# Block attention and a two-layer MLP: five rounds of 8, 8, 8, 6 and 6 token tiles in place of six of 6, W2 read from DRAM in each round, another order of products in a group

## Chip, cores, metric

One core of a Trainium2 chip runs the kernel. The metric is the time of one execution on the device in microseconds; lower is better.

## What is computed

Attention with a block-causal mask (blocks of 64 positions; 8 batches of 8 heads, 576 positions, head size 64), then layer norm, an MLP 512 -> 2048 -> 512 with ReLU, and the residual, in fp32:

```python
scores = scale * np.matmul(q, k.transpose(0, 1, 3, 2))
scores = np.where(block_i >= block_j, scores, -1000000000.0)
attn = np.exp(scores - np.max(scores, axis=-1, keepdims=True))
attn = attn / (np.sum(attn, axis=-1, keepdims=True) + 1e-09)
x = np.matmul(attn, v) ... reshaped to (8, 576, 512)
xn = (x - mu) / np.sqrt(var + 1e-06) * g_ln
out = x + np.maximum(xn @ w_ch1, 0.0) @ w_ch2
```

## The kernel before

The program is a list of tasks with dependencies, engines, estimated costs and priorities. `Plan.run` plays it through once while the kernel is built: at each moment every engine takes the ready task of lowest priority number whose buffers are free, and its instructions are emitted in that order. On the chip each engine then works through its own list in order; a task that waits holds up everything behind it on that engine. All loads and stores are issued from one list too, that of SyncE (SP). Buffers come from pools shared by several kinds of tile: `big`, `mid` and `small` (4, 9 and 15 buffers), with a most for each kind.

*Attention.* 32 pairs of heads (`pair`, priority 100 + 10 k). Per pair TensorE makes the scores (L394), VectorE adds the mask and takes the minimum (L409), ScalarE takes the exponential (L412), TensorE transposes the result (L421), a copy by ScalarE or VectorE (L216, L218) brings it to SBUF, TensorE multiplies by V (L427, L431), VectorE transposes (L504) and SyncE stores to the DRAM tensor `xd`. Four times `first` does the first 64 positions of eight pairs.

*Weights.* They arrive as 64-bit words; `decode` makes fp32 of them, 16 blocks of W1 and 16 of W2, from pair 12 on, the last ones well after attention. W1 goes to DRAM as fp32 (`w1f`); W2 is split into a high and a low part (two fp32r tiles whose sum is the weight) that stay in SBUF as `w2h` and `w2l`, 64 KB of each partition.

*Norm.* `norm_tiles(n, q)` takes two token tiles of 128: loads x from `xd` in four DMAs each, scales (L635), stores the row for the residual (L639), takes mean and variance (L644, L645), refines 1/sqrt on GpSimd (L662 and on), scales (L670, L673), transposes through VectorE and DRAM (L675, L679, L683) into `xt`. `operands(n)` forms from the three `xt` of a round the seven left operands `xm` of a seven-product scheme for a 2 x 2 block product, each split into high and low (L700 differences, L711 low parts).

*MLP.* 36 token tiles in six rounds of six. A round's tiles form two halves of three (384 tokens). Eight groups per round, each 256 hidden columns. In a group `products` computes the first layer by seven block products, 6 matmuls of 128x384 each, 42 in all (L803), from `wa` (products 1, 5, 2, 6) and `wb` (3, 7, 4). Products accumulate in three PSUM banks: `a` takes 1, 6, 7, 4, `d` takes 5, 3, `b` takes 2. ScalarE copies intermediate states to SBUF tiles t (L811), VectorE adds a later state to them (L816), then ScalarE (L822) and VectorE (L823) take the ReLU and split it into `h`. Product 4 continues in bank `a` and so waits until the addition to t5, which reads product 7 there, has ended. `second` multiplies `h` of the group before by W2, six matmuls 128x512 per token tile (L862), into a bank `y`, and VectorE adds it to the running sum `ya` (L871). The places of all these in a group are priorities written out by hand:

```python
p1 0, p5 14, p2 28, p6 30, p3 44, p7 58, p4 90
second: (7, 21, 37, 51, 65, 75)
```

`stream` brings `wa` and `wb`: in round 0 it builds them from `w1f` (GpSimd sums L762, splits L773) and stores them to `was` and `wbs`; in the later rounds it loads them, two buffers each. The norm work of round n + 1 runs under round n, gated by the first `h` of round n; that of round 0 runs under attention with the priority of pair 24 and no gate.

Of the kernel before, what the change touches and what calls it, by code (L numbers as in the profile page):

```python
# [26 lines left out]
TILES = 36  # L27
ROUND = 6
TN = 384
D_0, D_1 = 12.0, .97  # L30
LN_0 = 24
# [148 lines left out]
def pool(n):  # L180
    return .07 + n / 440

@with_exitstack
def attn_mlp_kernel(ctx: ExitStack, tc: tile.TileContext, qk, qk0, v, v0, w1, w2, g, out):
# [85 lines left out]
    new_v, new_word = mid("v", [P, 5, P], F32, 2), mid("wr", [P, 1024], I32, 2)  # L270
    new_h, new_xt = mid("h", [P, 2, 512], F32R, 6), mid("xt", [P, 2, 512], F32, 3)
# [3 lines left out]
    new_ya, new_x, new_xnt = (small(n, [P, 512], F32, k) for n, k in (("ya", 6), ("x", 2), ("xnt", 1)))  # L275
    new_t, new_tt, new_sum = small("t", [P, TN], F32, 4), small("tt", [P, 2, 2, P], F32, 3), small("sum", [P, 2, 256], F32, 2)
# [4 lines left out]
    w1f = [kind("w1f", [P, 2, 512], F32, NJ // 2, dram)() for _ in range(NJ // 2)]  # L281
    was, wbs = ([kind(n, [P, k], F32, NJ // 2, dram)() for _ in range(NJ // 2)] for n, k in (("was", 2048), ("wbs", 1536)))
# [4 lines left out]
    new_wf = kind("wf", [P, 2, 512], F32, 2, odd, "raw")  # L287
# [27 lines left out]
    w2b, w1b = {}, {}  # L315

    def decode(j, second, prio, gate):
# [29 lines left out]
        if not second:  # L347
            out = Buf(parent=w1f[j // 2])
            load(P * 2048, lambda: nc.sync.dma_start(out=w1f[j // 2].t[:, j % 2], in_=w()), r=[full], w=[out], prio=prio)
            w1b.setdefault(j // 2, []).append(out)  # L350
            return
        whole = w2s[j // 4]
        hb, lb = (Buf(parent=x) for x in whole)
        add(any_of(lambda e: copy(e, whole[0].t[:, j % 4], w()), ACT=act(n, True), DVE=.12 + n / 1920),
            r=[full], w=[hb], prio=prio)
        add(any_of(lambda e: e.tensor_sub(whole[1].t[:, j % 4], w(), whole[0].t[:, j % 4]), POOL=pool(n)),
            r=[full, hb], w=[lb], prio=prio)
        w2b[j] = [hb, lb]
# [243 lines left out]
    ROUNDS = TILES // ROUND  # L602
    HALF_R = ROUND // 2
# [4 lines left out]
    def norm_tiles(n, q, prio, gate):  # L608
# [4 lines left out]
        for h in range(2):  # L613
            t = ROUND * n + HALF_R * h + q
# [76 lines left out]
    def operands(n, prio):  # L691

        tts = [new_tt() for _ in range(HALF_R)]
# [24 lines left out]
        Q = range(HALF_R)  # L718
# [23 lines left out]
    def stream(n, gp):  # L742

        wa, wb = new_wa(), new_wb()
        if n == 0 and gp < 2:
            for x in (wa, wb):
                x.after.extend(big_of[NPAIR - 1, z] for z in range(2))
        if n:
            load(P * 8192, lambda: nc.sync.dma_start(
                out=wa.t.rearrange("p a b c -> p (a b c)").bitcast(F32), in_=was[gp].t), r=[stored[gp, 0]], w=[wa], prio=3)  # L750
            load(P * 6144, lambda: nc.sync.dma_start(
                out=wb.t.rearrange("p a b c -> p (a b c)").bitcast(F32), in_=wbs[gp].t), r=[stored[gp, 1]], w=[wb], prio=3)
            return (wa, [wa]), (wb, [wb])
# [125 lines left out]
    for n in range(ROUNDS):  # L879
# [68 lines left out]
```

## Time and profile before

| | |
|---|---|
| median of 3 runs | 1107.7 us (1102.53, 1107.7, 1108.54) |
| profiled execution | 1102.45 us, its span 1100.7 us, mean granted clock 0.994 |
| busy share of the span | TensorE 97%, VectorE 73%, ScalarE 42%, GpSimd 25% |
| matmuls of the MLP | 2016 of 128x384 (L803), 1728 of 128x512 (L862) |
| DMA | 213.32 MB, 62% of 16 engines' span |

The busy time of TensorE counts overlapping matmuls from start to modelled end, so it says that the engine had work, not at what pace; the pace is read from the starts of matmuls. The span is that of the profiled execution, and the time beside it includes what lies around the program.

### The profile page before, as it was taken

The page shows a single profiled execution, that of the slowest core. Times are in us where ns is not written, and L with a number is a line of the kernel's source. Part 1 is how long each engine was busy: PE and PEld are TensorE (multiplying, and loading weights), DVE is VectorE, ACT ScalarE, POOL GpSimd, SP SyncE. Part 2 cuts the span into 40 slices and gives each one's busy share as a digit, 9 for nine tenths or more (in the row PEclk, how much of TensorE's full clock was granted, in tenths as well). Part 3 has the DMA queues.
Part 4 walks back from the last instruction along what each step waited for, and adds up shares of the span by engine and source line. Part 5 has one row for each costly group of instructions (what it writes and reads, how often), then busy time and mean ns, then how long its engine had stood idle before and what let it go on. Part 6 is the DMA issues. An engine that isn't in the chain of part 4 may idle for free.

```text
span 1100.7 us, 18673 instructions
## 1 busy us (share of the span) xinstructions
PE 1065.7 (97%) x6576; PEld 902.7 (82%) x6576; DVE 804.1 (73%) x1797; ACT 464.0 (42%) x1154; POOL 275.2 (25%) x428
## 2 busy tenths in 40 slices
PE   9999999999989899999999999999999999999998
PEld 6777666777779788888889878888898888899887
DVE  6878988888889899776686665867667676754554
ACT  7778888898864332322132212321223221322221
POOL 0013726232265662212220212212201122200000
PEclk9999999999999999999999999999999999999999
DMA  5559696966678758777637675376665676463311
GB/s 182 152 174 248 228 241 227 288 210 201 216 280 269 214 167 249 229 209 190 210 121 258 171 203 154 132 249 179 180 197 169 220 186 185 160 228 116 134 68 58
DMA packets 232174, 213.32 MB, mean 194 GB/s; under 512 B 158736, under 2 KB 187408, under 8 KB 225936
## 3 DMA queue, kind: packets, MB, share of 16 engines
q1 hardware_dynamic: 232080, 212.12, 62.2%
q8 instruction: 52, 0.85, 0.3%
q14 instruction: 42, 0.34, 0.1%
HBM read 155.45 MB, written 56.62 MB: 193 GB/s over the span
## 4 chain that ended last, share of the span: by engine, by line
PE 56%; DVE 20%; DMA 9%; SPq 4%; issue 4%; ACT 3%; POOL 2%; DVEq 0%; POOLq 0%; ACTq 0%
PE y L862 21%; PE p L803 20%; PE s L394 4%; PE o L431 4%; PE tr L421 4%; DMA xt<-xw 3%; DMA x<-xd 3%; DVE ya L871 3%; DVE xm L711 2%; PE o L427 2%; DVE h L823 2%; DVE t L816 2%; DVE pab L409 2%; SPq L679 1%; DVE x L670 1%
## 5 line engine op out<-in xcount | busy, mean ns | idle before, releaser
L862 PE MATMUL y<-w2h,h 128*128 128x512 f32 x1152 | 398.8, 394 | 0.0
L871 DVE TENSOR_TENSOR ya<-y,ya 128x512 f32<-128x512 f32 x288 | 197.0, 684 | 115.2 <-PE y L862 114.9
L862 PEld LDWEIGHTS y<-w2h,h 128*128 128x128 f32 x1152 | 217.7, 189 | 39.1
L862 PE MATMUL y<-w2l,h 128*128 128x512 f32 x576 | 228.2, 396 | 0.0
L803 PE MATMUL p<-xm,wa 128*128 128x384 f32 x1152 | 225.4, 337 | 0.6 <-DVE ot L504 0.6
L822 ACT ACTIVATE h<-t 128x384 fp32r<-128x384 f32 x144 | 75.6, 525 | 336.0 <-DVE t L816 336.0
L803 PEld LDWEIGHTS p<-xm,wa 128*128 128x128 f32 x1152 | 205.3, 189 | 9.6 <-DVE ot L504 0.9
L803 PE MATMUL p<-xm,wb 128*128 128x384 f32 x864 | 176.6, 339 | 17.3 <-DVE t L816 12.9
L803 PEld LDWEIGHTS p<-xm,wb 128*128 128x128 f32 x864 | 153.6, 188 | 35.2 <-DVE t L816 19.3
L862 PEld LDWEIGHTS y<-w2l,h 128*128 128x128 f32 x576 | 108.7, 189 | 15.9
L811 ACT COPY t<-p 128x384 f32<-128x384 f32 x144 | 68.6, 476 | 116.8 <-PE p L803 104.2
L394 PE MATMUL s<-raw 64*128 64x320 f32 (+4 forms) x640 | 96.4, 437 | 1.7 <-DVE ot L504 0.8
L823 DVE SCALAR_TENSOR_TENSOR h<-t,h 128x384 fp32r<-128x384 f32 x144 | 81.9, 569 | 22.0 <-ACT h L822 21.9
L816 DVE TENSOR_TENSOR t<-p,t 128x384 f32<-128x384 f32 x144 | 79.1, 550 | 21.4 <-PE p L803 20.9
L412 ACT ACTIVATE pab<-pab,nm 128x576 f32<-128x576 f32 (+1 forms) x128 | 91.4, 725 | 4.1 <-DVE nm L409 4.0
L394 PEld LDWEIGHTS s<-raw 64*128 64x128 f32 x640 | 61.2, 188 | 37.7 <-issue 29.1
L409 DVE CUSTOM_DVE_ANT_0 pab<-s,never 128x576 f32<-128x576 f32 (+1 forms) x128 | 82.9, 683 | 3.5 <-PE s L394 3.0
L431 PE MATMUL o<-pt,v 128*64 128x256 f32 (+1 forms) x768 | 81.4, 347 | 0.0
L431 PEld LDWEIGHTS o<-pt,v 128*64 128x64 f32 x768 | 57.2, 139 | 27.2 <-issue 1.1
L412 ACT ACTIVATE pu<-pu,nm 128x320 f32<-128x320 f32 (+1 forms) x128 | 64.0, 503 | 28.9 <-DVE nm L409 27.6
L662 POOL TENSOR_TENSOR norm<-norm 128x2 f32<-128x2 f32 x54 | 12.4, 229 | 254.5 <-DVE norm L656 251.6
L421 PE MATMUL tr<-ident,pab 128*128 128x128 f32 x512 | 66.9, 276 | 9.1 <-ACT pt L216 4.9
(91 smaller groups left out, 1142.1 us busy)
## 6 DMA issues: line engine op xcount, KB each, us to landing
wa<-was SPq DMA_DIRECT2D x40, 1024.0 KB, 6.2
wb<-wbs SPq DMA_DIRECT2D x40, 768.0 KB, 5.0
raw<-qk SPq DMA_DIRECT2D x32, 576.0 KB, 4.5
wr<-w SPq DMA_DIRECT2D x32, 512.0 KB, 5.7
v<-v SPq DMA_DIRECT2D x32, 320.0 KB, 4.3
x<-xd SPq DMA_DIRECT2D x144, 64.0 KB, 3.0
xrow<-x SPq DMA_DIRECT2D x36, 256.0 KB, 4.1
xw<-xnt SPq DMA_DIRECT2D x144, 64.0 KB, 3.3
```

What stands on the lines that cost most here:

```text
L394: nc.tensor.matmul(x, raw.t[HALF[h], 0, col], raw.t[HALF[h], 1, at:at + x.shape[1]], start=True, stop=True)
L409: add("DVE", dve(n) + .01, lambda: nc.vector.tensor_tensor_reduce(out=p.t[:, part(i, h)], in0=s.t[:, cols], in1=hide, scale=-0.125, scalar ...
L412: add("ACT", act(n, True) + .14, lambda: nc.scalar.activation(out=p.t[:, part(i, h)], in_=p.t[:, part(i, h)], func=AF.Exp, bias=nm.t[:, at ...
L421: nc.tensor.transpose(o.t[:, n * P:(n + 1) * P], x, ident)
L431: nc.tensor.matmul(o.t[HALF[h], at + lo:at + 256], v_sb.t[:, ck, HALF[h]], rhs(h), start=False, stop=(n == len(steps) - 1), skip_group_che ...
L803: nc.tensor.matmul(x.t[:, 0:TN], w_(l), xs[m].t[:, :, o, k], start=start and k == e == 0, stop=k == 1 and e == 2, skip_group_check=True)
L811: add("ACT", act(TN), lambda: nc.scalar.copy(out=t.t, in_=x.t[:, 0:TN]), r=[r], w=[new], prio=0)
L816: add("DVE", dve(TN), lambda: nc.vector.tensor_add(t.t, x.t[:, 0:TN], t.t), r=r, w=[new], prio=0)
L822: add("ACT", act(TN, True), lambda: nc.scalar.activation(out=x.t[:, 0, 0:TN], in_=src(), func=AF.Relu), r=r, w=[hi], prio=0)
L823: add("DVE", dve(TN), lambda: nc.vector.scalar_tensor_tensor(out=x.t[:, 1, 0:TN], in0=src(), scalar=0.0, in1=x.t[:, 0, 0:TN], op0=ALU.max, ...
L862: nc.tensor.matmul(y, x.t[:, l, at:at + P], w.t[:, j % 4], start=i == e == 0, stop=i == 1 and e == 2)
L871: add("DVE", dve(512), lambda yb=yb, ya=ya: nc.vector.tensor_add(ya.t, yb.t, ya.t), r=[part, was_], w=[now], prio=1)
```

## The change

The 36 token tiles are taken in five rounds of 8, 8, 8, 6 and 6, so that a half is 512 tokens in three rounds and 384 in two. W2's high and low parts are no longer kept in SBUF: `decode` stores them to a DRAM tensor `wcs`, and `stream` loads a tile `wc` of 1 MB for each group of each round, with two buffers. The room that this frees goes to the pools (6, 13 and 21 buffers in place of 4, 9 and 15, shared by more kinds), to wider `xm`, and to more `ya`, `xt`, `xnt` and `tt`. In a group product 2 moves from third to sixth place, and the places of the second product are given for 6 and 8 tiles. The norm work of round 0 gets gates and priorities of its own, one pair of tiles at each of the pairs of heads 10, 13, 16 and 19. The loads of `w1f` for round 0 wait for earlier pairs, the first group's `wa` and `wb` need no longer wait for the last pair's buffers, and the very first product waits for the last pair's scores.

```diff
-ROUND = 6
-TN = 384
+ROUNDS = 8, 8, 8, 6, 6
-LN_0 = 24
+LN_0, LN_1 = 10, 3
...
-        return kind(name, shape, dtype, 4, None, "big", most)
+        return kind(name, shape, dtype, 6, None, "big", most)
...
-        return kind(name, shape, dtype, 9, None, "mid", most)
+        return kind(name, shape, dtype, 13, None, "mid", most)
...
-        return kind(name, shape, dtype, 15, None, "small", most)
+        return kind(name, shape, dtype, 21, None, "small", most)
+    new_wc = big("wc", [P, 2, 2, DM], F32R, 2)
+    new_wf, new_wd = mid("wf", [P, 2, 512], F32, 2), mid("wd", [P, 2, DM], F32R, 2)
-    new_h, new_xt = mid("h", [P, 2, 512], F32R, 6), mid("xt", [P, 2, 512], F32, 3)
+    new_h, new_xt = mid("h", [P, 2, 512], F32R, 6), mid("xt", [P, 2, 512], F32, 4)
-    new_ya, new_x, new_xnt = (small(n, [P, 512], F32, k) for n, k in (("ya", 6), ("x", 2), ("xnt", 1)))
+    new_ya, new_x, new_xnt = (small(n, [P, 512], F32, k) for n, k in (("ya", 10), ("x", 2), ("xnt", 2)))
-    w2s = [[kind(f"w2{x}{q}", [P, 4, DM], F32R, 1)() for x in "hl"] for q in range(4)]
-    xs = [kind(f"xm{p}", [P, ROUND // 2, 2, 2, P], F32R, 1)() for p in range(7)]
+    xs = [kind(f"xm{p}", [P, max(ROUNDS) // 2, 2, 2, P], F32R, 1)() for p in range(7)]
...
+        if second:
+            wd = new_wd()
+            hi, lo = Buf(parent=wd), Buf(parent=wd)
+            add(any_of(lambda e: copy(e, wd.t[:, 0], w()), ACT=act(n, True), DVE=.12 + n / 1920),
+                r=[full], w=[hi], prio=prio)
+            add("POOL", pool(n), lambda: nc.gpsimd.tensor_sub(wd.t[:, 1], w(), wd.t[:, 0]), r=[full, hi], w=[lo], prio=prio)
+            load(P * 4096, lambda: nc.sync.dma_start(
+                out=to.t[:, 1024 * (j % 2):1024 * (j % 2) + 1024], in_=wd.t.rearrange("p l n -> p (l n)").bitcast(F32)),
+                r=[hi, lo], w=[out], prio=prio)
...
-        wa, wb = new_wa(), new_wb()
+        wa, wb, wc = new_wa(), new_wb(), new_wc()
         if n == 0 and gp < 2:
-            for x in (wa, wb):
+            for x in (wa, wb, wc)[0 if gp else 2:]:
                 x.after.extend(big_of[NPAIR - 1, z] for z in range(2))
...
         if n:
+            for k in range(3):
+                fetch(k, 3)
+            return [(x, [x]) for x in (wa, wb, wc)]
...
-        load(P * 4096, lambda: nc.sync.dma_start(out=wf.t, in_=w1f[gp].t), r=[*w1b[gp], *late], w=[wf], prio=prio)
+        load(P * 4096, lambda: nc.sync.dma_start(out=wf.t.rearrange("p a n -> p (a n)"), in_=w1f[gp].t),
+             r=[*whole[False, gp], ends[NPAIR - 6 + gp % 2]], w=[wf], prio=prio)
+        fetch(2, 3)
...
-        p1 = product(1, a, True, [], [], 0)
+        p1 = product(1, a, True, [ends[NPAIR - 1]] if n == gp == 0 else [], [], 0)
         k1 = keep(t1, a, p1)
         p5 = product(5, d, True, [], [], 14)
         k5 = keep(t5, d, p5)
-        p2 = product(2, b, True, [], [], 28)
-        c11 = plus(b, t1, [p2, k1])
-        done[0, 0] = finish(0, 0, lambda: t1.t, [c11])
-        p6 = product(6, a, False, [p1], [p1], 30)
+        p6 = product(6, a, False, [p1], [p1], 28)
         k6 = keep(t6, a, p6)
-        p3 = product(3, d, False, [p5], [p5], 44)
+        p3 = product(3, d, False, [p5], [p5], 42)
...
-        p7 = product(7, a, False, [p6], [p6], 58)
+        p7 = product(7, a, False, [p6], [p6], 56)
...
-        p4 = product(4, a, False, [p7], [p7], 90)
+        p2 = product(2, b, True, [], [], 70)
+        c11 = plus(b, t1, [p2, k1])
+        done[0, 0] = finish(0, 0, lambda: t1.t[:, 0:TN], [c11])
+        p4 = product(4, a, False, [p7], [p7], 84)
...
+    PLACES = {6: (7, 21, 35, 49, 63, 77), 8: (7, 21, 35, 49, 61, 65, 77, 91)}
...
-                gate = hs[0, 0][1]
+                gate = hs[0][0, 1][1]
```

## Rows read from the trace of the kernel before

**Rows 1.** Busy time of each engine in six stretches of the execution (us from the start): the window, its length, then for each engine the busy us and in brackets the instructions; then the granted TensorE clock as a share of 2.4 GHz, the busy share of the 16 DMA engines and what they moved in GB/s. 103 to 320 lies in the attention part, 320 to 447 is round 0, 576 to 705 round 2, 834 to 962 round 4, 962 to 1088 the last round.
```profile
103.00:215.00 112.00, 104.96 (x1010) 75.78 (x1008) 99.53 (x287) 95.38 (x262) 55.99 (x68) 0.98 0.82 250
215.00:320.00 105.00, 101.77 (x947) 75.46 (x943) 86.73 (x248) 93.53 (x250) 36.95 (x32) 1.00 0.64 212
320.00:447.00 127.00, 119.41 (x579) 106.24 (x578) 116.45 (x212) 44.30 (x91) 68.56 (x90) 0.97 0.77 241
...
576.00:705.00 129.00, 126.14 (x624) 112.25 (x624) 88.29 (x174) 31.52 (x69) 25.04 (x54) 1.00 0.63 188
...
834.00:962.00 128.00, 125.49 (x624) 112.16 (x624) 88.56 (x173) 31.40 (x69) 24.16 (x52) 1.00 0.63 189
962.00:1088.00 126.00, 125.90 (x629) 113.16 (x628) 65.35 (x114) 27.98 (x58) 0.79 (x1) 1.00 0.34 119
```

**Rows 2.** The chain of work that ended last, in order of time, in the last round and to the end: start in us, length in us, what. A line gathers neighbours; the length of matmuls runs to the start of the next line.
```profile
1015.45 2.08 PE p L803 x12
1017.54 1.39 PE y L862 x6
...
1022.40 2.76 PE y L862 x12
1025.16 2.10 PE p L803 x12
...
1040.81 2.10 PE p L803 x12
...
1056.44 2.10 PE p L803 x12
...
1072.09 2.10 PE p L803 x12
...
1088.79 8.22 PE y L862 x36
...
1097.03 0.69 DVE ya L871
```

**Rows 3.** The same view over the whole execution, its longest pieces: the last product of the last group of a round together with the first product of the next round, for the first five rounds.
```profile
447.03 2.21 PE p L803 x12
...
576.09 2.35 PE p L803 x12
...
705.11 2.35 PE p L803 x12
...
833.84 2.35 PE p L803 x12
...
962.33 2.38 PE p L803 x12
```

**Rows 4.** TensorE in order of time where attention ends: start, length, engine, line, operation, out<-in, shape, count, and in brackets the idle time before it with what ended it.
```profile
314.87 1.33 PE L803 MATMUL p<-xm,wa 128*128 128x384 f32 x6
...
319.97 3.41 PE L803 MATMUL p<-xm,wa 128*128 128x384 f32 x18
...
326.03 1.32 PE L803 MATMUL p<-xm,wa 128*128 128x384 f32 x6 [0.56 <-DVE ot L504]
329.53 1.64 PE L803 MATMUL p<-xm,wb 128*128 128x384 f32 x6 [2.18 <-DVE t L816]
```

**Rows 5.** Whom TensorE waited for: the waiting line, the one waited for, us in total, times, longest. First round 0 (320 to 447), then all later rounds.
```profile
PE p L803 <- ACT t L811: 3.7, 1, 3.7
PE p L803 <- DVE t L816: 3.4, 3, 2.2
...
PE p L803 <- DVE t L816: 9.5, 7, 1.8
PE p L803 <- ACT t L811: 0.3, 1, 0.3
```

**Rows 6.** One of these waits in order of time, columns as in group 4: TensorE's product 7, then its product 4 (the last of the group); and VectorE in the same stretch.
```profile
651.83 1.21 PE L803 MATMUL p<-xm,wb 128*128 128x384 f32 x6
...
657.23 0.98 PE L803 MATMUL p<-xm,wb 128*128 128x384 f32 x4 [1.44 <-DVE t L816]
...
650.71 0.56 DVE L816 TENSOR_TENSOR t<-p,t 128x384 f32<-128x384 f32 x1 [0.42 <-PE p L803]
654.96 0.69 DVE L635 TENSOR_TENSOR x<-x,sums_all 128x512 f32<-128x512 f32 x1 [3.69 <-DMA x<-xd]
...
656.63 0.55 DVE L816 TENSOR_TENSOR t<-p,t 128x384 f32<-128x384 f32 x1
```

**Rows 7.** Three short stretches at two long waits, columns as in group 1.
```profile
377.00:382.00 5.00, 4.85 (x16) 4.12 (x17) 5.00 (x10) 2.06 (x5) 3.43 (x3) 0.66 0.72 224
...
525.00:527.20 2.20, 0.45 (x2) 0.02 (x1) 2.17 (x6) 0.00 (x0) 0.00 (x0) 1.00 0.94 305
527.20:532.00 4.80, 4.77 (x17) 4.43 (x18) 3.81 (x11) 1.50 (x3) 2.78 (x12) 0.64 0.86 335
```

**Rows 8.** DMA issues by destination and source: count, KB each, median us from issue to landing.
```profile
wa<-was SPq DMA_DIRECT2D x40, 1024.0 KB, 6.2
wb<-wbs SPq DMA_DIRECT2D x40, 768.0 KB, 5.0
...
wr<-w SPq DMA_DIRECT2D x32, 512.0 KB, 5.7
...
x<-xd SPq DMA_DIRECT2D x144, 64.0 KB, 3.0
```

More of the change, by code (lines that the diff above doesn't have):

```diff
@@ L311, in load @@
         add("SP", .6, fn, size=nbytes, **kw)
-    w2b, w1b = {}, {}
+    whole = {}
     def decode(j, second, prio, gate):
@@ L346, in decode @@
         w = lambda: sgn().bitcast(F32)
[L347 to L358, printed above, removed]
+        to = (wcs if second else w1f)[j // 2]
+        out = Buf(parent=to)
+        if second:
[7 more added lines that the diff above has]
+                r=[hi, lo], w=[out], prio=prio)
+        else:
+            load(P * 2048, lambda: nc.sync.dma_start(out=to.t[:, 512 * (j % 2):512 * (j % 2) + 512], in_=w()),
+                 r=[full], w=[out], prio=prio)
+        whole.setdefault((second, j // 2), []).append(out)
     FIRST = {4: 0, 3: 1152, 2: 0, 1: 640}
@@ L601, in attn_mlp_kernel @@
     END = 100 + 10 * NPAIR
-    ROUNDS = TILES // ROUND
-    HALF_R = ROUND // 2
+    FROM = [sum(ROUNDS[:n]) for n in range(len(ROUNDS))]
     GROUPS = NJ // 2
@@ L691, in operands @@
     def operands(n, prio):
-        tts = [new_tt() for _ in range(HALF_R)]
+        tts = [new_tt() for _ in range(ROUNDS[n] // 2)]
         got = {}
@@ L802, in go @@
                     for e, (l, o) in enumerate(((0, 0), (0, 1), (1, 0))):
-                        nc.tensor.matmul(x.t[:, 0:TN], w_(l), xs[m].t[:, :, o, k], start=start and k == e == 0,
+                        nc.tensor.matmul(x.t[:, 0:TN], w_(l), xs[m].t[:, 0:half, o, k], start=start and k == e == 0,
                                          stop=k == 1 and e == 2, skip_group_check=True)
             new = Buf(parent=x)
-            add("PE", 6 * MM, go, r=[*held[n, m], *wr, *r], w=[new, *w], prio=base + at)
+            add("PE", 6 * (TN / 2400 + MMO), go, r=[*held[n, m], *wr, *r], w=[new, *w], prio=base + at)
             return new
@@ L810, in keep @@
             new = Buf(parent=t)
-            add("ACT", act(TN), lambda: nc.scalar.copy(out=t.t, in_=x.t[:, 0:TN]), r=[r], w=[new], prio=0)
+            add("ACT", act(TN), lambda: nc.scalar.copy(out=t.t[:, 0:TN], in_=x.t[:, 0:TN]), r=[r], w=[new], prio=0)
             return new
@@ L843, in products @@
+        done[0, 0] = finish(0, 0, lambda: t1.t[:, 0:TN], [c11])
+        p4 = product(4, a, False, [p7], [p7], 84)
         done[1, 0] = finish(1, 0, lambda: a.t[:, 0:TN], [p4])
[L844 removed]
+        return {k: (hs[k], v) for k, v in done.items()}, ws[2]
     acc = {}
+    PLACES = {6: (7, 21, 35, 49, 63, 77), 8: (7, 21, 35, 49, 61, 65, 77, 91)}
     def second(n, gp, hs, base):
[L850 to L875 removed]
@@ L877, in attn_mlp_kernel, with go @@
-    late = [ends[NPAIR - 2]]
-    before, gate = None, []
-    for n in range(ROUNDS):
-        for q in range(HALF_R):
-            norm_tiles(n, q, 100 + 10 * LN_0 + q if n == 0 else END + 2 * n - 10, gate)
-        operands(n, 100 + 10 * LN_0 + 3 if n == 0 else 2)
+        hs, (wc, wr) = hs
+        half = ROUNDS[n] // 2
+        for place, s in zip(PLACES[2 * half], (*range(half, 2 * half), *range(half))):
+            yb = new_y()
+            t, h, at = FROM[n] + s, s // half, s % half * P
+            part = Buf(parent=yb)
+            def go(h=h, at=at, yb=yb):
+                for i in range(2):
+                    x = hs[i, h][0]
+                    for e, (l, o) in enumerate(((0, 0), (0, 1), (1, 0))):
+                        nc.tensor.matmul(yb.t, x.t[:, l, at:at + P], wc.t[:, i, o], start=i == e == 0, stop=i == 1 and e == 2)
+            add("PE", 6 * (512 / 2400 + MMO), go, r=[*final[NPAIR - 1], *hs[0, h][1], *hs[1, h][1], *wr], w=[part],
+                alloc=[yb], prio=base + place)
+            if gp == 0:
+                ya = new_ya()
+                load(P * 2048, lambda t=t, ya=ya: nc.sync.dma_start(out=ya.t, in_=xrow[t].t), r=[xparts_t[t]], w=[ya], prio=4)
+                acc[t] = ya, ya
+            ya, before_ = acc[t]
+            now = Buf(parent=ya)
+            add("DVE", dve(512), lambda yb=yb, ya=ya: nc.vector.tensor_add(ya.t, yb.t, ya.t), r=[part, before_], w=[now], prio=1)
+            acc[t] = ya, now
+            if gp == GROUPS - 1:
+                load(P * 2048, lambda t=t, ya=ya: nc.sync.dma_start(out=out[t], in_=ya.t), r=[now], w=[], prio=2)
@@ L883, in attn_mlp_kernel @@
+    before, gate = None, []
+    for n in range(len(ROUNDS)):
+        for q in range(ROUNDS[n] // 2):
+            norm_tiles(n, q, 100 + 10 * (LN_0 + LN_1 * q) if n == 0 else END + 2 * n - 10,
+                       gate if n else [ends[int(LN_0 + LN_1 * q) - 2]])
+        operands(n, 100 + 10 * (LN_0 + LN_1 * 4) if n == 0 else 2)
         for gp in range(GROUPS):
```

77 lines of the change are left out of this document (27 added, 50 removed).

## The prediction

> **What bounds the kernel now.** I read the busy time by stage first [rows 1]. TensorE is the busiest engine in every stage, but a busy TensorE is not one at its pace, so the next view is the chain of the last round, in which nothing is left to normalise: the same place of a group comes round at 1025.16, 1040.81, 1056.44 and 1072.09, so a group of 42 block-product matmuls and 36 of the second product takes 15.64 us, and the chain consists of matmuls alone [rows 2]. That is the floor of the second part: 48 groups x 15.64 = 750.7 us of TensorE.
>
> The chain of the whole execution shows the same place of the last group of each round: 447.03, 576.09, 705.11, 833.84, 962.33 [rows 3]. Rounds 1 to 4 thus take 515.3 us where 32 groups need 500.5: 14.8 us are lost. Round 0 begins at 319.97 with matmul runs not yet alternating with the second product [rows 4] and reaches its place at 447.03. It needs 42 matmuls at 0.173 (12 in 2.08 us [rows 2]), 7.3 us, then seven groups, less its first product (done at 314.87 [rows 4]) and its last: 7.3 + 109.5 - 2.1 = 114.7 of 127.1 us. So 12.4 us are lost there. The attention part takes 320 us before it.
>
> What the loss is: in rounds 1 to 5 TensorE waited 9.5 us, seven times, for the addition t on VectorE, in round 0 3.4 us for it and 3.7 us for a copy of ScalarE [rows 5]. One such wait from near: VectorE, an engine that works through its list in order, sits idle 3.69 us for a load of x from DRAM; behind that load's scaling stands the addition t, done at 657.2; only then does TensorE start the last product of the group, 1.44 us late by the idle column [rows 6]. VectorE is not full there (88.29 of 129 us [rows 1]); it is blocked. The longer of these waits cost more than their length: after the waits at 373 and 525 the granted clock is 0.66 and 0.64 for about 5 us, a mean between the two levels of 2.4 and 1.2 GHz [rows 7].
>
> **The change, part by part.**
>
> *Wider block products.* Columns stay equal (2016 x 384 = 1008 x 512 + 672 x 384); 336 matmuls go. A 384-column one takes 173.3 ns: 160 ns of columns at 2.4 GHz and 13.3 more. If the 13.3 stayed for 512 columns, one would take 226.7 ns, 4.4 ns less than four thirds of 173.3: 1008 x 4.4 = 4.4 us gained. The nearest row is the second product, already 128x512: 12 in 2.76 us are 230 ns, and the group's 15.64 leaves it 232.2, by which 1.2 us are lost. The range is -4.4 to +1.2; I take -1, nearer the 512-column rows. The Trainium skill ("TensorE: Matmul & The Clock Gate", section "Back-to-back issue gap") gives a warm gap of columns/2.4 ns plus 2.5 ns; by that 336 matmuls would return an estimated 0.8 us. The rows show 13.3 and 17 to 19 ns over the columns in place of 2.5, so the rule's fixed part isn't what these matmuls pay.
>
> *The order in a group.* The last product (4) needs the addition t5 that follows product 7. Before, two second-product blocks of 1.39 us lie between them, 2.8 us [rows 2]. Now product 2 is moved in between: y, y, 2, y in an 8-tile group, 3 x 1.39 + 1.39 = 5.6 us, and y, 2, y, 3.8 us, in a 6-tile group. In the wait above product 7 is through at about 652.9, the addition at 657.2: 4.3 us. An 8-tile group covers that wholly, a 6-tile group leaves 0.5 us. Of what else moved: product 6 now has 4.2 us behind product 1 (4.9 before) for a ScalarE copy, products 3 and 7 have 3.8; ScalarE is busy 31.52 of 129 us, so I cost that at nothing; without this cover it would be a repeat of round 0's 3.7. Product 2's result is needed in the next group's second half only.
>
> *Fewer, longer rounds.* The norm work in rounds 1 and later falls from 12 to 10 pairs of tiles, so without the new order 14.8 becomes 12.3. With it I leave one wait of about 1 us per round, 3.3 in all: -11.5 us. Bounds: -14 (all gone) and 0.
>
> *Round 0.* It grows from about 127 to 162 us, while decoding and building W1 in it stay the same; one more pair of tiles has to be normalised. VectorE: 116.45 of 127 us now [rows 1]; a last-round's 65.35 us are the products' share, four thirds of it less the missing first group is 82, the rest 55, the fourth pair 8: 145 of 162, 90% for 92%. So it stays tight. The two buffers more let W1 of the first group be built ahead of attention's end; that removes the 2.18 and 0.56 us waits of 326 and 329 [rows 4]; the new order covers the two t waits later, the ScalarE wait with its slow clock (3.7 and some 1.4) I leave. -5 us; bounds -10 and +2.
>
> *Attention: norm work moved in.* Round 0 has four pairs of tiles to prepare instead of three, under attention. The price of three pairs: stage 834 to 962 against the last round: VectorE 88.56 - 65.35 = 23.2, ScalarE 3.4, GpSimd 23.4 us [rows 1], per pair 7.7, 1.1 and 7.8. VectorE and ScalarE share PSUM copies, so 8.8 us spread over both are 4.4 us where both are full. They nearly are from 103 to 215 (VectorE 99.53, ScalarE 95.38 of 112), with 18 us of VectorE free from 215 to 320 [rows 1]. The new gates spread the pairs from pair 8 of heads to pair 19, within the full stage. The mid pool has 13 buffers in place of 9 for one more xt and two wd, which loosens the pairs of heads. I take +3, bounds -4 and +9.
>
> *W2 through DRAM.* Engine work is unchanged; 16 stores of 512 KB are new, some ten under attention by their priorities (0.97 of a pair apart from pair 12), and 40 loads of 1024 KB. Under attention this adds 5.2 MB in 200 us, 26 GB/s, 0.09 of share to 0.82 [rows 1]: loads land later than now, where weights take 5.0 to 6.2 us to land [rows 8]. +1, bounds 0 and +6. In the rounds a group loads 2816 KB instead of 1792 [rows 8]: by the last round's 119 GB/s at 0.34 and the norm work's 70 GB/s at 0.29, an 8-tile round comes to 208 GB/s at 0.68 and the 6-tile round with norm work to 254 GB/s at 0.82. A load has over a group's time (15.6 us or more) to land and takes 6.2: hidden. Without that cover each group would stop for some of the 6.2.
>
> *The end.* The last round still has six tiles, so its 36 last matmuls (8.22 us) and the 3.7 us to the end stay [rows 2].
>
> Sum: -1 - 11.5 - 5 + 3 + 1 = -13.5. The profiled execution took 1102.45 us (its span 1100.7 and 1.75 around it), which lies at the low end of the runs; so 1089.0 for a like one. The median is 1107.7, so I forecast 1094 us.
>
> **The rivals.**
> *The order doesn't cover* (15%). The wait turns to another neighbour: ScalarE's copies for products 6, 3 and 7, whose slack falls from 4.9 to 4.2 and 3.8. For it: ScalarE waits for t in order too, and one wait of 3.7 came so. Against it: in rounds 1 to 5 such waits are 0.3 us [rows 5]. Only -2.5 in place of -11.5 remains: 1103 us.
> *Attention fills up* (13%). The fourth pair lands in the full stage and the DMA share of 0.91 delays v and word loads: both at their upper bounds, +15 in place of +4: 1105 us.
> *Slower: the streams delay x* (12%). Its place is VectorE's wait for x in rounds 1 to 3. One 1 MB load more ahead of x on the same DMA engines costs what separates 6.2 from 3.0 us of landing [rows 8], so the 3.7 us wait becomes 6.9, past the covers of 5.6 and 3.8. Beyond about 5 us of blocking it decides. 20 tiles at about 2 us are 40 us instead of the 3.3 left: 1094 + 37 = 1131; at half the tiles 1113. Against it: a share of 0.68 leaves room; for it: 305 and 335 GB/s stood where the longest wait of 525 ended [rows 7].
> *Attention gains* (5%): the larger pools end its buffer waits, -4 in place of +4, with the 4.4 of the matmuls: 1083 or less.
>
> **How the numbers follow.** The forecast has 55%, in a range of its own from 1083 to 1102. No change means within 0.5% (5.5 us), about what a measurement here can tell. Faster: 53 of the forecast's 55, 6 of the first rival, 4 of the second, and 5 of the last: 68%. Slower: 1 + 2 + 2 + 9 = 14%. Same: 18%. The range from 1080 to 1113 leaves out the slower rival and little else.
>
> **What would show it.** Right: groups of 20.7 to 21.0 us in the first three rounds and 15.64 in the last two; block products of 512 columns at 227 to 232 ns; waits of TensorE for t in later rounds under 4 us in all; first steady block product at 320 to 326; W2 loads landing in 6 to 8 us with no TensorE wait on them. Wrong: TensorE idle behind a DMA or behind ScalarE's copies in rounds 1 to 3, an attention part over 330 us, or a round 0 losing more than 12 us.

## The result, and the profile after

The changed kernel takes 1071.15 us (median of 4 runs, 1069.32 to 1074.17) where the kernel before took 1105.12 beside it: a ratio of 0.9699, interval 0.9648 to 0.975. Two more measurements gave 1068.49 with 0.9701 (0.9676 to 0.9725) and 1070.13 with 0.9716 (0.9692 to 0.9739). The direction was forecast; the size was not: 1071 lies below the whole range of 1080 to 1113, and a gain of 34 us stands against a forecast of 13.5.

The profiled execution took 1069.32 us (span 1067.5) against 1102.45 (span 1100.7). Its stages, columns as in [rows 1]: round 0, the two other rounds of eight tiles, the round of six with norm work, the last round:

```profile
317.00:478.00 161.00, 157.22 (x682) 127.97 (x679) 137.54 (x240) 60.23 (x116) 93.52 (x118) 0.99 0.85 278
478.00:641.00 163.00, 163.00 (x721) 135.01 (x720) 115.66 (x213) 39.00 (x78) 40.53 (x76) 1.00 0.70 220
641.00:805.00 164.00, 164.00 (x727) 136.14 (x726) 105.81 (x190) 37.02 (x71) 24.00 (x52) 1.00 0.65 207
805.00:930.00 125.00, 125.00 (x623) 111.97 (x622) 82.75 (x162) 27.38 (x60) 23.04 (x52) 1.00 0.80 256
930.00:1055.00 125.00, 124.89 (x622) 111.52 (x621) 65.19 (x112) 27.94 (x63) 3.21 (x4) 1.00 0.50 184
```

From 478 to 1055 TensorE is idle for 0.1 us; of 127 us in round 0 it was without work for 7.6 in [rows 1], now for 3.8 of 161, some of the rest at a lower clock.

The chain of waits (start, length, what), answering [rows 2]: the same place of a group in rounds of eight tiles, then in the last round of six:

```profile
487.69 2.72 PE y L874 x12
490.41 1.36 PE p L814 x6
...
508.09 2.72 PE y L874 x12
...
793.69 2.72 PE y L874 x12
...
1023.33 2.08 PE p L814 x12
1025.41 1.39 PE y L874 x6
...
1038.97 2.08 PE p L814 x12
...
1055.65 8.22 PE y L874 x36
```

From 487.69 to 793.69 the place comes round every 20.40 us, 15 times without an exception. Six matmuls of 512 columns take 1.36 us, 226.7 ns each, block products and second products alike. In the last round it is the old 15.64, with 1.39 for six second products. The 36 last matmuls and the 3.6 us behind them are as before.

Whom TensorE waited for in the whole execution (columns as in [rows 5]):

```profile
PE y L874 <- ACT h L833: 1.8, 1, 1.8
...
PE p L814 <- DVE wb L784: 1.5, 1, 1.5
...
PE p L814 <- DVE t L827: 0.2, 1, 0.2
```

The waits for the addition t, 12.9 us in [rows 5], are 0.2. Where attention ends, answering [rows 4]: the first steady block products start at 317.06 instead of 319.97, with no wait behind them.

```profile
317.06 3.06 PE L814 MATMUL p<-xm,wa 128*128 128x512 f32 x12
319.95 2.88 PE L814 MATMUL p<-xm,wb 128*128 128x512 f32 x12
```

DMA issues, as in [rows 8]: W2's loads land in 6.8 us, the others a little later than before.

```profile
wc<-wcs SPq DMA_DIRECT2D x40, 1024.0 KB, 6.8
wa<-was SPq DMA_DIRECT2D x32, 1024.0 KB, 7.6
...
x<-xd SPq DMA_DIRECT2D x144, 64.0 KB, 3.8
```

**Where 33.2 us of span went.** Groups: 48 of 15.64 were 750.7 us; 24 of 20.40 and 16 of 15.64 are 739.8, so 10.9 less. What TensorE lost above the pace: round 0 12.4 before, 7.5 now; the later rounds 15.1, now 0.7. Attention ends 2.9 earlier. Together 10.9 + 4.9 + 14.4 + 2.9 = 33.1.

| step | forecast | between the two profiles |
|---|---|---|
| pace of the matmuls | -1 (-4.4 to +1.2) | -10.9 |
| waits of later rounds | -11.5 (-14 to 0) | -14.4 |
| round 0 | -5 (-10 to +2) | -4.9 |
| attention, norm work and W2's stores | +4 | -2.9 |
| the end | 0 | -0.1 |

**What is left in round 0.** TensorE in order of time, then ScalarE, VectorE and SP's queue, each with the idle time before the instruction in brackets:

```profile
450.49 6.33 PE L874 MATMUL y<-wc,h 128*128 128x512 f32 x18 [1.81 <-ACT h L833]
...
460.74 4.24 PE L874 MATMUL y<-wc,h 128*128 128x512 f32 x18
...
447.25 0.63 ACT L215 CAST wa<-wf 128x512 fp32r<-128x512 f32 x1 [11.55 <-DMA wcs<-wd]
449.28 1.67 ACT L833 ACTIVATE h<-t 128x512 fp32r<-128x512 f32 x3 [1.41 <-DVE t L827]
...
439.29 0.69 DVE L636 TENSOR_TENSOR x<-x,sums_all 128x512 f32<-128x512 f32 x1 [2.12 <-DMA x<-xd]
441.77 0.69 DVE L636 TENSOR_TENSOR x<-x,sums_all 128x512 f32<-128x512 f32 x1 [1.79 <-DMA x<-xd]
...
448.57 0.68 DVE L827 TENSOR_TENSOR t<-p,t 128x512 f32<-128x512 f32 x1
...
431.52 7.82 SPq L627 DMA_DIRECT2D x<-xd  x8
...
440.47 0.43 SPq L765 DMA_DIRECT2D wf<-w1f  x1
```

ScalarE sat 11.55 us ahead of a cast whose data are loaded by the issue at 440.47 (6.8 us to landing; the view names a store issued just after it), and this issue stood in SP's list behind eight loads of x that took 7.82 us to issue. Behind the cast the activation h waited another 1.41 us, for an addition t on VectorE, which had itself stood 2.12 and 1.79 us for the same loads of x and worked without a gap from 441.77 on. So both engines that h needs were held up by these eight loads. The wait of 1.81 us then cost more than its length: 18 matmuls take 6.33 us where 18 take 4.24 ten us later, and the granted clock from 450.5 to 455.5 is 0.66, a mean between the two levels, as in [rows 7].

### The profile page after: what moved, and what is told of

The parts are those of the page before. It is cut to its first block, busy times and chain, and to the rows that moved or that the text cites. A ratio compares the mean times of both kernels' runs of the same rounds, so it can differ in the third digit from the quotient of the medians.

```text
span 1067.5 us, 17862 instructions
## 1 busy us (share of the span) xinstructions
PE 1049.8 (98%) x6240; PEld 856.0 (80%) x6240; DVE 789.0 (74%) x1726; ACT 450.2 (42%) x1099; POOL 292.4 (27%) x442
## 4 chain that ended last, share of the span: by engine, by line
PE 55%; DVE 5%; POOL 2%; DMA 2%; issue 1%; SPq 1%; ACT 0%; DVEq 0%; POOLq 0%
PE y L874 30%; PE p L814 25%; DVE h L834 1%; DVE ya L883 1%; SPq L627 1%; DMA wcs<-wd 1%; DMA wc<-wcs 1%; DVE t L827 0%; POOL x L674 0%; DVE xnt L676 0%; DVE xm L712 0%; DVE wb L784 0%; DVE wa L784 0%; DVE st L645 0%; DVE sgn L342 0%
## 5 line engine op out<-in xcount | busy, mean ns | idle before, releaser
L874 PE MATMUL y<-wc,h 128*128 128x512 f32 x1728 | 438.0, 392 | 2.1 <-ACT h L833 1.8
L874 PEld LDWEIGHTS y<-wc,h 128*128 128x128 f32 x1728 | 323.7, 188 | 66.4 <-DVE h L834 2.5
L814 PE MATMUL p<-xm,wa 128*128 128x512 f32 (+1 forms) x960 | 222.5, 368 | 0.1
L833 ACT ACTIVATE h<-t 128x512 fp32r<-128x512 f32 (+1 forms) x120 | 62.4, 581 | 275.9 <-DVE t L827 265.9
L814 PE MATMUL p<-xm,wb 128*128 128x512 f32 (+1 forms) x720 | 167.5, 368 | 1.7 <-DVE wb L784 1.5
L822 ACT COPY t<-p 128x512 f32<-128x512 f32 (+1 forms) x120 | 65.3, 545 | 192.6 <-PE p L814 189.2
L827 DVE TENSOR_TENSOR t<-p,t 128x512 f32<-128x512 f32 (+1 forms) x120 | 75.8, 632 | 42.5 <-PE p L814 40.1
L396 PE MATMUL s<-raw 64*128 64x192 f32 (+4 forms) x640 | 96.5, 435 | 1.3 <-DVE nm L411 0.6
L834 DVE SCALAR_TENSOR_TENSOR h<-t,h 128x512 fp32r<-128x512 f32 (+1 forms) x120 | 76.9, 694 | 0.3 <-ACT h L833 0.2
L215 ACT COPY pt<-tr 128x512 f32<-128x512 f32 (+1 forms) x126 | 65.0, 580 | 3.1 <-PE tr L423 2.7
```

Source lines behind the costliest of these rows:

```text
L215: e.copy(out=out, in_=in_)
L396: nc.tensor.matmul(x, raw.t[HALF[h], 0, col], raw.t[HALF[h], 1, at:at + x.shape[1]], start=True, stop=True)
L814: nc.tensor.matmul(x.t[:, 0:TN], w_(l), xs[m].t[:, 0:half, o, k], start=start and k == e == 0, stop=k == 1 and e == 2, skip_group_check=True)
L822: add("ACT", act(TN), lambda: nc.scalar.copy(out=t.t[:, 0:TN], in_=x.t[:, 0:TN]), r=[r], w=[new], prio=0)
L827: add("DVE", dve(TN), lambda: nc.vector.tensor_add(t.t[:, 0:TN], x.t[:, 0:TN], t.t[:, 0:TN]), r=r, w=[new], prio=0)
L834: add("DVE", dve(TN), lambda: nc.vector.scalar_tensor_tensor(out=x.t[:, 1, 0:TN], in0=src(), scalar=0.0, in1=x.t[:, 0, 0:TN], op0=ALU.max, ...
```

## The experiments

Theory A: the gain is one of matmul pace, because a 512-column product costs columns at 2.4 GHz plus a fixed 13.3 ns, and the second product pays more than that only beside narrower ones. Theory B: the gain is one of waits; order, pools and rounds keep the streams apart. Each run below undoes one part or does one part alone; where nothing else is said, it is an edit of the changed kernel. Since the lists are planned anew for each kernel, they also differ from some point on (with six tiles from 80 us, with the extra load from 142, with nine mid buffers from 285, with the old order from 320), so a single wait can come from the new lists as well as from the part undone.

**Six tiles per round, all else kept.**

```
-ROUNDS = 8, 8, 8, 6, 6
+ROUNDS = 6, 6, 6, 6, 6, 6
```

> The changed kernel with six rounds of six tiles, all else kept (W2 from DRAM, pools, new order, gates). Theory A, the width is worth about 11 us by pace: groups at 15.64 us, second product at 231 to 232 ns, rounds 1 to 4 losing under 3 us in all, time about 1080 to 1084 us where the changed kernel took 1069 to 1074. Rival, the wider rounds are what ended the waits: rounds 1 to 4 lose 10 us or more and the time is 1090 or above.

Measured: 1108.78 us, 1.0066 (1.0044 to 1.0088) of the kernel before: with everything but the rounds kept, the gain is gone and a little more. The pace alone explains 11 of the 38 us. TensorE's waits:

```profile
PE p L814 <- DVE xm L217: 19.1, 1, 19.1
...
PE p L814 <- DVE xm L712: 3.1, 3, 1.6
PE y L874 <- DMA wc<-wcs: 2.7, 1, 2.7
...
PE p L814 <- DVE t L827: 1.5, 2, 0.9
```

One wait of 19.1 us, at 448, for the operands xm of round 1: the preparation of the second round was not done when the first ended. Two windows, round 0 and the stretch of that wait, and the chain just ahead of it:

```profile
320.00:450.00 130.00, 123.98 (x606) 109.86 (x604) 110.06 (x207) 44.95 (x96) 59.15 (x80) 0.99 0.89 302
447.50:467.00 19.50, 0.76 (x4) 0.29 (x2) 3.82 (x9) 0.00 (x0) 4.86 (x14) 0.64 0.89 287
...
445.95 5.57 DMA xrow<-x
...
454.42 6.31 DMA xw<-xnt
...
462.48 3.24 DMA xw<-xnt
...
465.87 2.96 DMA xt<-xw
```

No engine is busy for more than 4.9 of the 19.5 us of the wait, and the DMA engines stand at 0.89. The norm chain goes through DRAM (x in, xrow and xw out, xt back in), each hop with a transfer on DMA engines that W2's stream now shares. Preparing round 1 under round 0 thus takes longer here than a first round of six tiles lasts; in the changed kernel, with one of eight, it is through at about the border, near 478. The later rounds pay nothing like it: from 580 to 970 the DMA share is 0.80 at 257 GB/s, and all of TensorE's waits from 490 on come to 2.2 us.

**The old order of a group**, in the changed kernel.

```
+        p2 = product(2, b, True, [], [], 28)   # c11 and finish with it
+        p6 = product(6, a, False, [p1], [p1], 30)
...
+        p7 = product(7, a, False, [p6], [p6], 58)
...
-        p2 = product(2, b, True, [], [], 70)   # c11 and finish with it
-        p4 = product(4, a, False, [p7], [p7], 84)
+        p4 = product(4, a, False, [p7], [p7], 90)
...
-    PLACES = {6: (7, 21, 35, 49, 63, 77), 8: (7, 21, 35, 49, 61, 65, 77, 91)}
+    PLACES = {6: (7, 21, 37, 51, 65, 75), 8: (7, 21, 29, 37, 45, 51, 65, 75)}
```

> The changed kernel with product 2 back in third place, so that two second-product blocks (2.7 us) lie between products 7 and 4; rounds and all else kept. Theory A, the order ended the waits for the addition t: TensorE waits for t of 1 to 2 us return in rounds 1 to 3, 8 to 12 us in all, time 1078 to 1084. Rival, the larger pools (x, xnt, xt) ended them: under 2 us return, time 1069 to 1075.

Measured: 1088.21 us, 0.9886 (0.9844 to 0.9927), 17 to 20 us more than the changed kernel. TensorE's waits:

```profile
PE p L814 <- DVE xm L217: 10.7, 1, 10.7
PE p L814 <- DVE t L827: 6.3, 4, 2.0
```

The waits for t are back, and round 1's operands come 10.7 us late, at 485. Before that wait it is not DRAM that holds the preparation up: VectorE is busy for 21.86 of the 22 us from 453 to 475, and only then are the last stores of xw issued. Round 0 has its eight tiles here, so its length alone does not hide the preparation of round 1.

**The new order in the kernel before**, nothing else; the gate of the norm work is set one finish later, since product 2 comes later.

```
-        p2 = product(2, b, True, [], [], 28)   # c11 and finish with it
...
+        p2 = product(2, b, True, [], [], 70)   # c11 and finish with it
...
-        p4 = product(4, a, False, [p7], [p7], 90)
+        p4 = product(4, a, False, [p7], [p7], 84)
...
-                    alloc=[yb], prio=base + (7, 21, 37, 51, 65, 75)[2 * pair_ + z])
+                    alloc=[yb], prio=base + (7, 21, 35, 49, 63, 77)[2 * pair_ + z])
...
-                gate = hs[0, 0][1]
+                gate = hs[0, 1][1]
```

> The kernel before with the new order in a group alone (product 2 sixth, second product at 7, 21, 35, 49, 63, 77). If the order ended the waits: rounds 1 to 4 lose under 5 us where the kernel before lost 14.8, time 1088 to 1096 us. If the pools did: they lose 10 us or more and the time is within 4 us of the kernel before.

Measured: 1084.84 us, 0.9842 (0.9789 to 0.9895); the span is 1084.8 against 1100.7. TensorE's waits in the whole execution:

```profile
PE p L803 <- DVE t L816: 2.5, 2, 1.5
PE y L862 <- DVE h L823: 1.9, 2, 1.6
PE p L803 <- ACT t L811: 1.3, 1, 1.3
```

All of them stand in round 0; from 448 on the view of waits has no entry at all. So the order alone, without the larger pools, is worth some 16 us and ends every wait of the later rounds.

**Order and gates in the kernel before**: the edit above, and the gates of round 0's norm work (the edit of "the gates alone", below). Beside the changed kernel with six tiles this lacks the stream of W2, the larger pools, and the looser conditions of round 0's loads and buffers of W1.

> The kernel before with the new order and the gates of round 0's norm work, six tiles per round, W2 held in SBUF. It differs from the changed kernel with six tiles per round only in the streaming of W2 and in the pools. If the stream of W2 is what makes the preparation of round 1 late there (19.1 us at the border), this kernel waits under 2 us for round 1's operands, and takes 1080 to 1086 us, like the order alone (1084.84). If the gates, which put norm work of round 0 later, are what makes it late, 10 us or more of that wait stand here and the time is 1092 to 1105 us.

Measured: 1083.66 us, 0.9835 (0.9811 to 0.986). At the border of rounds 0 and 1 the view of waits has no entry from 440 to 460, and the DMA share of round 0 is 0.75 where it was 0.89 with six tiles and the stream. So neither the gates nor the order make round 1's operands late; the stream does, or else the pools or the loads of W1, which no run tells apart from it. For the stream speak the 302 GB/s of round 0 with six tiles, against 234 here: eight loads of 1 MB in 130 us are 65 GB/s.

**Both taken out**: six tiles per round and the old order, in the changed kernel (the two edits above together).

> Six rounds of six with the old place of product 2 in the otherwise changed kernel (W2 from DRAM, larger pools, gates). Compared with the same kernel with the new order, whose rounds 1 to 4 lost few us (single waits up to 1.4 us, most at the borders): if the order ended the waits for t, TensorE waits for t of 8 us or more in all return in rounds 1 to 4. If the larger pools ended them (one xnt and one xt more), under 4 us return.

Measured: 1111.37 us, 1.0075 (1.0045 to 1.0106). Waits for t are 5.7 us in five, the border costs 18.4, W2's load 3.7. The old order costs 3 us at most here (1108.78 without it, and the two intervals overlap). An explanation that fits, not tested further: where the border waits for the preparation anyway, time saved on TensorE ahead of it is given back there.

**What a matmul costs beside another.** A kernel of matmul streams alone, with nothing of the reference: 384 columns alone, 512 alone, six and six in turn as in the kernel, then other widths, and last the two one by one.

```
for r in range(12):
    for e in range(6): mm(a[:, 0:384], W(e), strided(3)(e), ...)
    for e in range(6): mm(b[:, 0:512], W(e), y(e), ...)
```

> Only streams of matmuls (fp32r, weights 128x128 changed at each), nothing of the reference: 384 columns alone; 512 alone; blocks of six of 384 (strided, then contiguous) with blocks of six of 512; six strided 512 with six 512; six 256 with six 512; six 448 with six 512; 384 and 512 one by one. Theory C, a neighbour of another width costs the 512-column ones: 226.7 ns alone and beside strided 512, 231 to 232 beside 384, strided or not. Rival, the stride of the moving operand does it: 226.7 beside contiguous 384 and 231 beside strided 512.

Measured from start to start, at a granted clock of 1.00: alone, 384 columns take 173.4 ns and 512 take 226.8, both columns at 2.4 GHz and 13.4 more. The chain: 512 alone, 512 beside 384, and beside 512 read as four strided blocks.

```profile
33.20 32.68 PE b L43 x144
...
65.88 1.06 PE a L46 x6
66.94 1.39 PE b L48 x6
...
124.30 1.37 PE a L56 x6
125.67 1.36 PE b L58 x6
...
157.67 1.39 PE b L63 x6
```

Counted from the first start of a block to that of the next, the 512 beside 384 columns take 231.6 ns each and the 384 take 174.0 to 174.3, strided or not; beside 256 columns it is 231.2 and 118.8, beside 448 it is 230.2 and 202.0, and with 512 and 384 one by one 231.4 and 175.2. Beside its own width a 512 takes 226.8. So the extra 3.5 to 5 ns belong to the mixture of widths, not to the second product; theory A holds for the pace.

**W2 loaded twice** in rounds 1 to 4: its third load is issued again into the same tile.

```
-            for k in range(3):
+            for k in (0, 1, 2, 2):
```

> The changed kernel with each W2 tile of rounds 1 to 4 loaded twice, 1 MB more per group. If the DMA has the room that its busy share (0.65 to 0.80) says, rounds 1 and 2 stay without a wait of TensorE (20.40 us a group) at a share near 0.9, and only round 3 (0.80 before) shows waits: 1069 to 1080 us. The rival of the prediction, that streams delay x and VectorE with it: waits for t in all of rounds 1 to 3, 1085 us or more.

Measured: 1137.42 us, 1.0307 (1.0265 to 1.0349). SP's waits, the queue that issues the loads:

```profile
SPq L758 <- DMA wc<-wcs: 219.7, 32, 11.4
SPq L758 <- PE p L814: 109.1, 33, 12.8
```

The second copy has to wait until the first has landed, and all that stands behind it in SP's list waits too. TensorE's longest waits:

```profile
PE p L814 <- DVE xm L217: 22.5, 2, 18.9
PE p L814 <- DVE xm L712: 9.7, 2, 7.9
```

They stand at the borders of rounds 1 and 2 (664 to 677) and of rounds 3 and 4 (986 to 1006): here the operands of rounds 2 and 4 come late. With the list held for 219.7 us, the run does not tell what the additional traffic alone would cost.

**An extra load of 512 KB per group** in rounds 1 to 4, into a tile of its own that nothing reads.

```
+            more = new_more()
+            load(P * 4096, lambda: nc.sync.dma_start(out=more.t, in_=wcs[gp].t[:, 0:1024]), ..., prio=3)
```

> The changed kernel with half a W2 tile (512 KB) more loaded per group of rounds 1 to 4, into a tile of its own that nobody reads, so that no load waits for another. If the doubled load was slow through its wait in SyncE's list (219.7 us in all, 32 waits for the first load to land), here, at a DMA share near 0.78 and 0.90, rounds 1 and 2 stay at 20.4 us a group and the time is 1068 to 1078 us. If the bandwidth is what it ran into, waits of TensorE come back in rounds 1 to 3 and the time is 1085 us or more.

Measured: 1097.88 us, 0.9954 (0.9928 to 0.998). The 32 loads in SP's list (duration, first and last start), TensorE from 485 on (bracket: idle time), and windows of rounds 1 and 2:

```profile
L764 SPq DMA_DIRECT2D more<-wcs x32: 319/440/1249, 141.7 to 619.4; - x32
...
503.37 0.77 PE L817 MATMUL p<-xm,wa 128*128 128x512 f32 x1 [17.73 <-ACT xm L215]
507.62 2.90 PE L817 MATMUL p<-xm,wa 128*128 128x512 f32 x6 [3.48 <-DVE xm L713]
...
490.00:655.00 165.00, 145.87 (x620) 119.68 (x621) 98.72 (x180) 32.53 (x61) 29.14 (x65) 0.92 0.84 260
655.00:815.00 160.00, 159.89 (x705) 132.05 (x705) 104.75 (x186) 37.01 (x73) 28.14 (x56) 1.00 0.65 210
```

The loads did not fall where they were meant to. Since nothing held them back, the first was issued at 141.7 us, under attention, and the last at 619.4, in round 1. Rounds 2 to 4 had none, and round 2 moves what it moves in the changed kernel (210 GB/s against 207); so what more traffic would cost the later rounds isn't shown. The loss is the border of round 0 once more, where eight of these loads stand in SP's list between 439 and 501, among the loads of x and the stores of xw: the fourth pair's last transpose into xnt starts at 488.7 in place of 458.9. Attention also ended later, at 324.9, with the first extra loads in its lists.

**The attention part.** Three edits: round 0's norm work at once after pair 24 instead of spread by gates; the mid pool of 9 buffers; W2's stores closer together.

```
-            norm_tiles(n, q, 100 + 10 * (LN_0 + LN_1 * q) if n == 0 else END + 2 * n - 10,
-                       gate if n else [ends[int(LN_0 + LN_1 * q) - 2]])
-        operands(n, 100 + 10 * (LN_0 + LN_1 * 4) if n == 0 else 2)
+            norm_tiles(n, q, 100 + 10 * 24 + q if n == 0 else END + 2 * n - 10, gate)
+        operands(n, 100 + 10 * 24 + 4 if n == 0 else 2)
```

> The changed kernel with the norm work of round 0 as before: priority of pair 24, no gate; all else kept. Theory B, the gates are why attention did not grow: the first block products in a row begin 4 to 8 us later than the 317.1 of the changed kernel. Rival, the larger pools are why: they begin within 1.5 us of it.

Measured: 1094.51 us, 0.9935 (0.9908 to 0.9962). Attention ends at 329.9, and round 1's operands are 15.5 us late at 493.

```
-        return kind(name, shape, dtype, 13, None, "mid", most)
+        return kind(name, shape, dtype, 9, None, "mid", most)
```

> The changed kernel with 9 mid buffers in place of 13. Theory B (gates): attention ends within 2 us of the changed kernel's 317.1. Rival (pools): attention ends 4 to 10 us later. In round 0 both expect some loss, since h, wr, wd, wf and xt share 9 buffers there.

Measured: 1076.59 us, 0.9765 (0.9739 to 0.9791). Attention ends at 326.2; up to 284 us the lists of VectorE and ScalarE and their times are those of the changed kernel, so what it loses (4 to 11 us by the spread given below) comes in its last stretch.

```
-D_0, D_1 = 12.0, .97
+D_0, D_1 = 12.0, .90
```

> The changed kernel with decodes 0.90 of a pair apart in place of 0.97. Round 0 lost about 7 us in the changed kernel, over 4 of them where the second product waited 2.2 us for a W2 tile just stored at 441 to 449 us and then ran at half clock. If that is it, this wait goes and the time falls by 2 to 5 us. Rival: the earlier decodes lengthen attention by as much, no change.

Measured: 1075.49 us, 0.9747 (0.9718 to 0.9777). Attention ends at 322.2. The wait at 448 that it was to remove is gone: TensorE has no wait from 330 to 473. But between 474 and 477 it waits 1.8 us in three for h, and 3.4 us in two for the operands of round 1, up to 491. So the loss moved to the end of the round, and the time did not fall.

**The gates alone, in the kernel before.**

```
-            norm_tiles(n, q, 100 + 10 * LN_0 + q if n == 0 else END + 2 * n - 10, gate)
-        operands(n, 100 + 10 * LN_0 + 3 if n == 0 else 2)
+            norm_tiles(n, q, 100 + 10 * (10 + 3 * q) if n == 0 else END + 2 * n - 10,
+                       gate if n else [ends[int(10 + 3 * q) - 2]])
+        operands(n, 100 + 10 * 22 if n == 0 else 2)
```

> The kernel before with the gates and priorities of round 0's norm work alone (pairs 10, 13, 16 instead of 24 without a gate), three pairs of tiles. If the gates shorten attention by themselves, block products in a row begin 4 to 12 us before the 320.0 of the kernel before. If they only undo what the fourth pair costs, they begin within 3 us of 320.0.

Measured: 1097.44 us, 0.9958 (0.9935 to 0.998). Attention ends at 319.8, where it ended before. On three pairs of tiles the gates gain nothing in attention. A few us came in the rounds: the wait of 3.7 us in round 0 for a copy of ScalarE [rows 5] is 0.6, and the waits for t from 448 on are 7.1 us in place of 9.5.

**The changed kernel again**, twice, for its own spread.

> The changed kernel again, beside the next one on the same chip: 1068 to 1075 us, a ratio of 0.967 to 0.973.

> The changed kernel again, as the other side of that comparison: 1067 to 1072 us.

Measured: 1068.49 and 1070.13 us, with the ratios given above. In the profile of the first repeat attention ends at 319.8, 2.7 us later than in the profile above, with the same lists, and in that of the second at 318.2. The run with W2 loaded twice, whose lists are the same up to there, has 321.7, and the three of the next experiment, the same up to there too, have 316.1, 318.4 and 315.3. So the end of attention wobbles by 6 us over seven executions, and the -2.9 of the table lies within that. Of the runs on attention 329.9 and 326.2 are clear of it.

**More of the same width**: four rounds of eight tiles and one of four, run three times, on two chips.

```
-ROUNDS = 8, 8, 8, 6, 6
+ROUNDS = 8, 8, 8, 8, 4
...
+    PLACES = {4: (7, 35, 63, 91), ...
```

> Rounds of 8, 8, 8, 8 and 4 tiles. Theory A and C: 32 groups at 20.4 us, and eight of 42 x 256 columns and 24 x 512: 256 columns at 120 ns (106.7 and 13.3) and 512 at about 231 give 10.6 us a group, in sum 2 to 3 us less than the changed kernel. If the 256-column ones are bound by something else (weight loads), at 140 ns or more, 4 us more than it.

> Rounds of 8, 8, 8, 8 and 4 again. By the stream measurement, 8 groups of 90 matmuls at 226.7 ns and 8 of 42 at 119 and 24 at 232 ns (247.8 us) stand for 16 groups of 15.64 (250.2 us), and one round border less work: 2 to 4 us below the changed kernel.

> Four rounds of eight tiles and one of four, a third time, beside the changed kernel on this chip. By the durations of the groups 2.4 us below the changed kernel; if the price of the shorter last round is paid elsewhere, no difference.

Measured: 1067.17 us, 0.9682 (0.9643 to 0.9721); 1065.78, 0.9678 (0.9654 to 0.9701); 1066.74, 0.969 (0.9665 to 0.9715). The second ran on one chip with the changed kernel's 1068.49, the third on one with its 1070.13: 2.7 and 3.4 us less, and of the third no run (1063.47 to 1069.03) reaches the changed kernel's lowest beside it (1069.90). By the durations above, 32 groups of 20.40 us and eight of 42 x 0.119 + 24 x 0.232 = 10.57 give 737.3, 2.5 less than 739.8, which agrees. It is a version that beats both kernels, the changed one by 0.3%.

## Why the prediction was wrong in size

**Pace: the step that failed.** "I take -1, nearer the 512-column rows" chose between two rows, and the choice was wrong: the second product's 230 to 232 ns [rows 2] were read as the price of 512 columns, but they are the price of 512 columns beside 384. With one width throughout, 226.7 ns hold for block products (1008 x 4.4 ns = 4.4 us, the step's best case) and for the second product as well (24 groups x 48 x 5.55 ns = 6.4 us). The sum is measured; how it splits hangs on whether a 384-column product beside the others is put at 173.3 ns or at the 174.0 to 174.3 of the streams, which makes the shares about equal. The second share stood in no bound: an operation that the change doesn't touch was taken as fixed. This is 10 of the 20 us that the forecast missed.

**Waits of the later rounds: right in mechanism and near in size.** The order covers the addition; the wait that was left per round did not come, so 14.4 us instead of 11.5 by this table, just past the bound of -14 (the loss was put at 14.8, and this table counts 0.3 of the last round with it). The order alone, in the kernel before, ended these waits and took 15.9 us off the span, round 0's share with it. That "a 6-tile group leaves 0.5 us" was too careful: none is left in the six-tile groups of that kernel's rounds 1 to 5.

**Round 0: right**, -4.9 for -5, with the ScalarE wait and its low clock left as assumed (it is another such wait, behind SP's list). What the step did not see is that round 0 must also cover the preparation of round 1. In the changed kernel, at 161 us, it just fits; at 129 us, with six tiles, it costs 19.1 us, and at eight tiles the old order, the ungated norm work or the extra loads each make it late as well, by 10.7 to 17.7 us. What holds it up differs: hops through DRAM with six tiles, VectorE's list with the old order, SP's list among others with the extra loads. The step's condition, VectorE's share, is thus one of several.

**Attention: wrong in sign, within what can be told.** +4 was forecast and -2.9 seen, with a wobble of 6. A price is there: without the gates attention ends 9.9 us later than before, with the fourth pair and W2's stores in it, between the two terms' 4 and their upper bounds of 15. The gates, for which nothing was counted, take it back, and the pool of 13, which was noted as loosening but given no number, is worth 4 to 11 us at the end of this part. What W2's loads put on the DMA engines in the rounds came as estimated: 207 GB/s at 0.65 and 256 at 0.80.

**The rivals.** "The streams delay x" (12%) has its mechanism in these kernels, but at another place than the forecast put it: not as waits for t in rounds 1 to 3 but as one wait for round 1's operands, at the border of rounds 0 and 1, of 10.7 to 19.1 us in five of them, and with W2 loaded twice for those of rounds 2 and 4. The changed kernel is spared it: with another order, six tiles per round or no gates it comes. With six tiles per round it would have decided: 1.0066 and 1.0075. "The order doesn't cover" and "attention fills up" did not come. "Attention gains" gave 1083 or less, but by another way: its pace share is there, its attention share is within the wobble.

**Sum of the parts.** Order alone in the kernel before: -15.9 of span, with the gates -18.9. Pace: -10.9. The rest, 3 to 6 us, is not assigned: attention's 2.9, and what stream, pools and gates do in round 0, are no larger than the spread between two profiles. Loading W2 gains nothing by itself: with six tiles per round, the new order and the gates, 0.9835 of the kernel before became 1.0066 with the stream, the pools and the loads of W1. It makes the room for rounds of eight tiles.

What stays open: why mixed widths cost the wide matmul 3.5 to 5 ns (the streams show that, not by what), what more traffic would cost the later rounds, and how much room the border of round 0 has left in the changed kernel.

## What to carry to other kernels

Before a matmul's duration is used as that of its width, look at what stands beside it in the stream: a row of an operation that the change leaves alone can still move when its neighbours change. Put independent work between a product and the one that waits for its post-processing, by the length of that wait in the trace; here it gave half of the gain without any memory. And when loads are added, ask which stage must prepare the next one under them and whether it still can: the long waits appeared at borders of rounds, where the next round's operands were not ready.

## What the runs showed of the hardware that was not expected

A 128x128 by 512-column fp32r matmul with its weights changed each time takes 226.8 ns in a stream of one width and 230.2 to 231.6 in turn with narrower ones (448, 256, 384); whether the narrower operand is strided makes no difference (384). The 13.4 ns above the columns are the same for 384 and 512 alone. The Trainium skill ("TensorE: Matmul & The Clock Gate", section "Back-to-back issue gap") states 2.5 ns over the columns as the isolated warm gap; these streams do not show it, and here too the measurement decides.

Eight loads of x occupied SP's queue for 7.82 us, one of them for 3.45, and what stood behind them in its list was issued that much later. In the run with W2 loaded twice one repeated load per group held the list for 219.7 us in all, while the DMA engines' share was 0.75 to 0.79 in the windows from 500 to 980.
